# A new hand-over order and a new choice of engines for the 2,407 works of an attention and two-layer expert kernel

## The chip, the cores and the metric

The kernel runs on one core of a Trainium2 chip. The metric is the device time of one launch in microseconds. Before the change it is 660.46 us, the median of three runs (659.9 to 663.03).

## The reference: what is computed

Attention over 4 batches of 8 heads, 576 positions and 64 columns per head: heads 0 to 3 look at the last 32 positions, heads 4 to 7 at every fourth of the last 128. Its output, 2,304 tokens by 512, goes through a layer of 1,024 columns with a SoLU and a layer norm, and through a second one of 2,048 columns with a sigmoid GELU. All in float32; the four expert weights come as float64.

```python
scores = np.where(masks, q @ k.T / 8, -1e9)
x = softmax(scores) @ v                       # to (2304, 512)
h = x @ w_in;   s = h * softmax(h)
y = ((s - mean(s)) / sqrt(var(s) + 1e-6) * g_ln) @ w_out
h2 = y @ w2_in; g = h2 * sigmoid(1.702 * h2)
out = g @ w2_out
```

## The kernel before

**Works and queues.** The kernel body does not issue instructions as it goes. It fills a `Plan` (lines 61 to 163) with 2,407 works by `add` (line 67): an engine, a cost in us, a function that issues the instructions, the works it comes after, and the buffers it takes and gives back. A work can have further engines (`also`); which of them it gets is PICKS[number] (0, the first, where nothing stands). ORDER is a list of all work numbers written out by hand, found by a search outside of the kernel. `in_order` (line 78) walks it, gives every work a start time by the costs in the code, and `emit` (line 150) issues the works in order of these times, chained per engine in that order. So on each of TensorE, VectorE, ScalarE, GpSimd and SP (which issues every DMA) the works run strictly in the order in which ORDER names those of that engine; a work whose operands are late holds up all behind it on its engine. Works on GpSimd, and VectorE works marked `port`, also follow one another in the planner's times, as both read through a shared port.

**Attention** is 20 units (`n` = 5 x batch + u): u = 0 to 3 are two heads each with 512 positions, u = 4 the last 64 positions of all heads. A unit goes through `att_s` (scores, TensorE, line 258), `att_max` and `att_sub` or `att_mask` (VectorE), `att_exp` (ScalarE, line 318), `att_sum` (three VectorE instructions, lines 339 to 341), `att_norm` (GpSimd, for some VectorE, line 344), `att_t` (transposition, TensorE, line 348), `att_p` (copy out of PSUM, ScalarE or VectorE, line 357), `att_x` (times v, line 362) and two `att_y` copies.

**First expert layer.** 18 tiles of 128 tokens. Float32 products are made of three products of split operands: a rounded high part and the rest, the low part (`moe_xh`, line 505, and `moe_xl`, line 511, for tokens; `split_hi`, line 477, and `split_lo`, line 490, for weights, which `to_f32_*` first turns from float64 to float32). `moe_h` (line 517) is two halves of twelve products; then come maximum, exponential, SoLU, mean, variance and norm (`moe_ln`, GpSimd), the transposition `moe_lt` (line 572) and `moe_y` (line 593), 24 products for each of four column blocks of six groups of three tiles.

**Second expert layer.** Three passes (p = 0 to 2) of 768 tokens, by a scheme with seven products for a 2 x 2 block (m = 0 to 6) in both matrix products. Its weights ("units", 32 of them) are fetched, converted, summed (`unit_sum`), split (`unit_hi`, `unit_lo`) and stored to DRAM during the first layer, and loaded back per pass (`quad_load`, `o_load`, `o_load2`; the tiles ws, wo and w). `y_sum` (line 691), `y_hi` (line 700) and `y_lo` (line 705) make the seven token operands of a pass. `h_prod` (line 710) and `o_prod` (line 785) are six TensorE instructions each; `o_sum` (line 754), `o_hi` (line 761) and `o_lo` (line 765) make the operands of `o_prod` from the GELU's output; `h_u2` to `h_c12` add the products up in VectorE.

**Dummy products.** In the attention and in `moe_h` a helper issues bf16 products that nobody reads, as many as the planner's gap ahead of the work says:

```python
def stir(bank):
    x = ident_b.rearrange("p (o n) -> p o n", o=1).broadcast_to([P, 4, P])
    for _ in range(min(4, int(STIR * plan.gap / 4))):      # STIR = 7
        nc.tensor.matmul(bank.rearrange("p (o n) -> p o n", o=4), ident_b, x, start=True, stop=True)
```

The lines that take the order and the choice of engine:

```python
pick = PICKS.get(len(self.works), 0) if ORDER else pick           # line 70
one = [list(can)[pick]] if pick >= 0 else list(can)
for k, n in enumerate(ORDER):                                     # line 81
    w = self.works[n]
    (w.eng, (w.cost, w.fn, port)), = w.can.items()
```

Of the kernel before, what the change touches and what calls it, by code (L numbers as in the profile page):

```python
# [60 lines left out]
class Plan:  # L61
# [5 lines left out]
    def add(self, rank, eng, cost, fn, after=(), take=(), give=(), lag=None, also=(), port=False, pick=-1):  # L67
        lag = {"PE": 0.2, "POOL": 0.1}.get(eng, 0.06) if lag is None else lag
        can = {eng: (cost, fn, port and eng != "ACT" or eng == "POOL")}
        can.update({e: (c, f, port or e == "POOL") for e, c, f in also})  # L70
        pick = PICKS.get(len(self.works), 0) if ORDER else pick
        one = [list(can)[pick]] if pick >= 0 else list(can)
# [31 lines left out]
    def order(self):  # L104
        if ORDER:
            return self.in_order()
# [1179 lines left out]
def plan_sequence():  # L1286
# [29 lines left out]
    for b in range(1, B):  # L1316
        todo, k = items[b - 1], 0
        for u in range(UB):
# [47 lines left out]
ORDER = [8, 1, 56, 57, 58, 59, 4, 77, 0, 46, 78, 79, 47, 48, 60, 61, 80, 81, 49, 50, 5, 67, 68, 9, 266, 82, 83, 10,  # L1366
# [245 lines left out]
```

## Time and profile before

| | |
|---|---|
| median of three runs | 660.46 us (659.9 to 663.03) |
| the profiled execution | 656.88 us |
| its span, first to last instruction | 655.1 us |
| TensorE busy | 632.4 us, 97% of the span |
| VectorE, ScalarE, GpSimd busy | 448.4, 353.8 and 307.1 us |
| DMA | 163.53 MB, 250 GB/s in the mean |
| chain that ended last | TensorE 81%, VectorE 6%, DMA 5% |

How to read it: busy times overlap, so TensorE's 97% says that the end is set by what lies between its products, and where. The busy time of an engine with a lower share matters only where another engine waits for it. A line "A <- B" in the list of waits gives how long engine A stood until B released it.

### The profile page before, as it was taken

Reading aid. Unit: us, or ns where it says so; the run is one execution under the profiler, and the core shown is the slowest. Engines: PE = TensorE matmul, PEld = TensorE weight load, DVE = VectorE, ACT = ScalarE, POOL = GpSimd, SP = SyncE. Lnnn points to the kernel's source line nnn. Section 1 sums busy time; section 2 is a strip of 40 time slices with the busy share of each in tenths; the row PEclk is TensorE's granted clock in tenths of the full one; section 3 lists DMA queues with packets and bytes.
Section 4 is the critical chain, followed back from the end, with each engine's and each line's share of the span. In section 5 each row is a group of like instructions: output and inputs, shape, how many; then the busy total and the mean of one; then the engine's idle time right before and its main releaser. Section 6 shows DMA issues by size and latency. Waiting matters only on the chain.

```text
span 655.1 us, 14276 instructions
## 1 busy us (share of the span) xinstructions
PE 632.4 (97%) x5587; PEld 590.4 (90%) x5587; DVE 448.4 (68%) x736; ACT 353.8 (54%) x757; POOL 307.1 (47%) x348
## 2 busy tenths in 40 slices
PE   6799999999999999999999999999999999999997
PEld 3467889888989899999999999999999899999997
DVE  4898987685686857577877879434577754265663
ACT  4778884664475675645556755224456432334552
POOL 2347575665664485552554034302547730134671
PEclk9899999999999999999999999999999999999999
DMA  8895943743326755887899998667789768868873
GB/s 328 332 349 219 333 160 111 272 157 124 138 111 226 252 197 187 294 310 262 284 333 345 339 351 300 194 227 256 250 284 313 265 219 246 287 203 300 273 246 109
DMA packets 65011, 163.53 MB, mean 250 GB/s; under 512 B 6960, under 2 KB 28592, under 8 KB 64944
## 3 DMA queue, kind: packets, MB, share of 16 engines
q1 hardware_dynamic: 64944, 162.62, 72.4%
q8 instruction: 44, 0.72, 0.4%
q14 instruction: 23, 0.19, 0.1%
HBM read 126.42 MB, written 36.18 MB: 248 GB/s over the span
## 4 chain that ended last, share of the span: by engine, by line
PE 81%; DVE 6%; DMA 5%; issue 3%; POOL 2%; ACT 1%; SPq 1%; ACTq 0%; DVEq 0%; POOLq 0%
PE y L599 15%; PE h L525 15%; PE hz L720 14%; PE oz L798 10%; PE hx L720 10%; PE ox L798 8%; PE lt L579 3%; DMA wo<-wdo 2%; DVE gs L766 2%; PE s L271 2%; PE xt L384 1%; PE xt L387 1%; DMA v<-in_v_dram 1%; PE ptp L354 1%; DMA wdo<-hl_('o', 3, 1)_1_4964 1%
## 5 line engine op out<-in xcount | busy, mean ns | idle before, releaser
L763 ACT CAST gs<-g 128x384 fp32r<-128x384 f32 x168 | 84.9, 513 | 73.9 <-PE oz L798 33.9
L766 POOL TENSOR_TENSOR gs<-g,gs 128x384 fp32r<-128x384 f32 x59 | 67.2, 1143 | 98.2 <-ACT gs L763 87.3
L720 PE MATMUL hz<-yc,ws 128*128 128x384 f32 x492 | 98.5, 335 | 0.5 <-DVE u L732 0.3
L599 PE MATMUL y<-ln_t,wo_h 128*128 128x384 f32 x384 | 98.6, 337 | 0.0
L766 DVE TENSOR_TENSOR gs<-g,gs 128x384 fp32r<-128x384 f32 x109 | 74.4, 699 | 33.5 <-ACT gs L763 33.0
L720 PEld LDWEIGHTS hz<-yc,ws 128*128 128x128 f32 x492 | 86.3, 188 | 1.6 <-DVE u L732 1.0
L759 POOL TENSOR_TENSOR g<-g,g 128x384 f32<-128x384 f32 x38 | 42.2, 1117 | 80.2 <-ACT g L749 51.8
L720 PE MATMUL hx<-yc,ws 128*128 128x384 f32 x369 | 74.8, 335 | 0.6 <-DMA ws<-wdq 0.5
L599 PEld LDWEIGHTS y<-ln_t,wo_h 128*128 128x128 f32 x384 | 68.9, 188 | 0.5
L720 PEld LDWEIGHTS hx<-yc,ws 128*128 128x128 f32 x369 | 64.8, 188 | 1.2 <-DMA ws<-wdq 0.8
L599 PE MATMUL y<-ln_t,wo_l 128*128 128x384 f32 x192 | 64.3, 335 | 0.0
L749 ACT ACTIVATE g<-g 128x384 f32<-128x384 f32 x72 | 36.1, 521 | 51.8 <-DVE g L739 21.2
L525 PE MATMUL h<-wi_h,xh 128*128 128x512 f32 x144 | 59.0, 409 | 0.0
L798 PE MATMUL oz<-gs,w 128*128 128x384 f32 x288 | 53.9, 338 | 3.0 <-DVE gs L766 3.0
L525 PE MATMUL h<-wi_h,xl 128*128 128x512 f32 x144 | 56.6, 393 | 0.0
L525 PE MATMUL h<-wi_l,xh 128*128 128x512 f32 x144 | 56.3, 391 | 0.0
L798 PE MATMUL oz<-gs,wo 128*128 128x384 f32 x288 | 55.2, 337 | 1.0 <-DMA wo<-wdo 0.9
L798 PE MATMUL ox<-gs,wo 128*128 128x384 f32 x288 | 55.1, 338 | 0.7 <-DMA wo<-wdo 0.7
L798 PEld LDWEIGHTS oz<-gs,w 128*128 128x128 f32 x288 | 50.0, 188 | 4.1 <-DVE gs L766 3.6
L798 PEld LDWEIGHTS oz<-gs,wo 128*128 128x128 f32 x288 | 50.2, 188 | 2.2 <-ACT hl_('o', 3, 0)_0_4868 L654 0.7
L798 PEld LDWEIGHTS ox<-gs,wo 128*128 128x128 f32 x288 | 50.2, 188 | 1.6 <-DMA wo<-wdo 1.0
L759 DVE TENSOR_TENSOR g<-g,g 128x384 f32<-128x384 f32 x58 | 40.4, 701 | 14.0 <-POOL gs L766 8.2
(415 smaller groups left out, 1216.7 us busy)
## 6 DMA issues: line engine op xcount, KB each, us to landing
wo<-wdo SPq DMA_DIRECT2D x48, 512.0 KB, 5.8
ws<-wdq SPq DMA_DIRECT2D x41, 512.0 KB, 5.6
w<-wdo SPq DMA_DIRECT2D x72, 256.0 KB, 5.6
ws<-wdq SPq DMA_DIRECT2D x41, 384.0 KB, 5.4
qk<-in_qk_dram SPq DMA_DIRECT2D x14, 528.0 KB, 5.8
v<-in_v_dram SPq DMA_DIRECT2D x14, 512.0 KB, 6.7
out_dram<-ob SPq DMA_DIRECT2D x11, 384.0 KB, 5.8
w_t<-in_w_in_dram SPq DMA_DIRECT2D x8, 512.0 KB, 9.4
```

What stands on the lines that cost most here:

```text
L271: nc.tensor.matmul(ps[QB * j:QB * j + QB, h, m * KW:m * KW + KW], q_[rows, c:c + QB], k_[rows, c:c + KW], start=not masked, stop=not maske ...
L354: nc.tensor.transpose(ps[:, j * P:j * P + P], t[:, 2 * j:2 * j + 2, :].rearrange("p m k -> p (m k)"), ident)
L384: nc.tensor.matmul(o, w, pt[rows, x:x + QB].rearrange("p (r t) -> p r t", r=4), start=True, stop=True, tile_position=(64 * par, 64 * h))
L525: nc.tensor.matmul(hps[i][:, half, :], x[:, kt, :], w[:, kt, fs], start=(kt == 0 and j == 0), stop=(kt == KT - 1 and j == 2))
L579: nc.tensor.transpose(ps[:, j, :], es[i][:, f * P:f * P + P], ident)
L599: nc.tensor.matmul(yps[g, dm][:, 0:TG].rearrange("p (t n) -> p t n", t=GT), w[:, f, ds_], x[:, :, f, :], start=(f == 0 and j == 0), stop=( ...
L720: nc.tensor.matmul(ps[:, 0:TB2], quad_weights(p, q, m, kk, a), yc2[m][:, x, kk, :], start=(m < 4 and kk == 0 and i == 0), stop=(kk == 1 an ...
L749: nc.scalar.activation(g_tile(q, 0, 0) if (half, b) == (0, 0) else src, src, AF.Gelu_apprx_sigmoid)
L759: eng.tensor_tensor(o_block(jj, *o), o_block(jj, *x), o_block(jj, *y_), op)
L763: nc.scalar.copy(gsp[jj, m][:, 0], o_block(jj, half, b))
L766: eng.tensor_tensor(gsp[jj, m][:, 1], o_block(jj, half, b), f32(gsp[jj, m][:, 0]), ALU.subtract)
L798: nc.tensor.matmul(ps, w, gsp[jj, m][:, x], start=m < 4 and first and i == 0, stop=last and i == 2, skip_group_check=True)
```

## The change

The lists ORDER and PICKS are replaced, and nothing else. No cost, dependency, buffer or function changes, so both kernels issue the same works. The heads of the lists, and the lines around the end of pass 1:

```diff
-ORDER = [8, 1, 56, 57, 58, 59, 4, 77, 0, 46, 78, 79, 47, 48, 60, 61, 80, 81, 49, 50, 5, 67, 68, 9, 266, 82, 83, 10,
-         97, 98, 267, 268, 269, 69, 70, 14, 71, 3, 262, 261, 6, 84, 85, 86, 263, 18, 7, 62, 272, 99, 264, 265, 271,
...
-         1961, 1962, 1934, 1960, 1963, 1924, 1920, 1921, 1918, 1922, 1964, 1965, 1966, 1979, 1935, 1906, 1907, 1980,
-         1981, 1908, 1868, 1940, 1947, 1925, 1926, 1990, 1992, 1984, 1985, 1986, 1936, 2033, 2030, 1937, 1996, 2031,
...
-PICKS = {75: 1, 76: 1, 95: 1, 96: 1, 115: 1, 136: 1, 144: 1, 160: 1, 171: 1, 179: 1, 190: 1, 193: 1, 204: 1, 215: 1,
...
+ORDER = [1, 8, 56, 57, 58, 59, 18, 87, 88, 89, 0, 46, 60, 61, 4, 9, 77, 47, 48, 90, 49, 62, 50, 51, 78, 10, 97, 52, 7,
+         53, 91, 266, 267, 268, 79, 80, 81, 82, 6, 272, 5, 67, 54, 269, 270, 63, 98, 83, 68, 55, 271, 99, 273, 69, 70,
...
+         1913, 1916, 1966, 1924, 1925, 1926, 1917, 1974, 1975, 1950, 1980, 1981, 1985, 1986, 1989, 2010, 1990, 1992,
+         1982, 1936, 1937, 1996, 1987, 1943, 1993, 1994, 1995, 2001, 1997, 2031, 1998, 1999, 2003, 2033, 2034, 1946,
...
+PICKS = {50: 1, 52: 1, 54: 1, 55: 1, 73: 1, 86: 1, 91: 1, 104: 1, 127: 1, 136: 1, 146: 1, 159: 1, 160: 1, 168: 1,
...
```

Read with the works' numbers: 0 to 45 are loads (8 is query 1, 1 the masks, 18 the last block of batch 0). 1908, 1917 and 1926 are `o_prod` of pass 1, m = 5, for groups 1, 3 and 5; 1925 is the `o_lo` that 1926 needs; 1980 and 1985 are `y_sum` 2 and 3 of pass 2; 1992, 1996, 1994, 2001, 1998 and 2003 are `h_prod` 0, 2, 1, 4, 3 and 5 of its first quad, and 1982 and 1987 the `y_lo` for products 3 and 5.

Works by engine: VectorE 674 before and 711 after, ScalarE 612 and 592, GpSimd 286 and 269, TensorE 496 and SP 321 both times.

| works | GpSimd to VectorE | VectorE to GpSimd | ScalarE to VectorE | VectorE to ScalarE | to GpSimd from ScalarE |
|---|---|---|---|---|---|
| `o_lo` (168) | 37 | 25 | | | |
| `o_sum` (96) | 28 | 11 | | | |
| `unit_sum` (128) | 26 | 30 | | | |
| `unit_lo` (64) | 12 | 19 | | | |
| `y_lo`, `y_sum` (33) | 10 | 2 | | | |
| `unit_hi` (64) | | 2 | 10 | 3 | 9 |
| `att_p`, `att_y` (60) | | | 16 | 11 | |
| `moe_lnh`, `moe_yc` (60) | | | 15 | 14 | |

The number of dummy products follows from the gaps that `in_order` finds: 25 before, 34 after.

## Rows read from the trace of the kernel before

**Rows 1.** Windows by stage: us, busy (count) PE, PEld, DVE, ACT, POOL; granted clock, DMA share, GB/s
```profile
20.00:60.00 40.00, 33.94 (x826) 25.69 (x827) 37.83 (x52) 29.80 (x58) 20.96 (x20) 0.91 0.86 327
60.00:276.00 216.00, 216.00 (x2311) 193.21 (x2309) 157.56 (x272) 136.54 (x311) 130.04 (x182) 1.00 0.56 193
0.00:60.00 60.00, 46.73 (x1176) 33.15 (x1177) 46.24 (x68) 39.45 (x90) 25.09 (x31) 0.91 0.88 332
300.00:400.00 100.00, 97.72 (x555) 95.77 (x554) 78.69 (x139) 57.60 (x117) 40.08 (x44) 1.00 0.94 325
530.00:652.00 122.00, 120.72 (x687) 118.52 (x685) 64.87 (x106) 48.88 (x103) 42.92 (x40) 1.00 0.75 240
```
**Rows 2.** TensorE's waits: who for whom; us in total, times, longest
```profile
PE oz L798 <- DVE gs L766: 3.0, 2, 2.6
...
PE oz L798 <- DMA wo<-wdo: 0.9, 2, 0.5
PE ox L798 <- DMA wo<-wdo: 0.7, 1, 0.7
```
**Rows 3.** Windows in the start, columns as in rows 1
```profile
0.00:38.00 38.00, 27.10 (x732) 17.84 (x732) 26.01 (x39) 22.51 (x56) 13.12 (x17) 0.87 0.89 329
28.00:30.00 2.00, 0.13 (x2) 0.10 (x1) 2.00 (x3) 0.81 (x4) 0.00 (x0) 1.00 0.14 45
32.00:34.00 2.00, 2.00 (x91) 2.00 (x85) 1.86 (x8) 1.96 (x2) 0.61 (x1) 0.50 1.02 401
```
**Rows 4.** TensorE's timeline in the start: start, us, instruction [idle before, releaser]
```profile
30.38 0.38 PE L253 MATMUL xt<-ident_b 128*128 128x512 bf16 x1 [2.26 <-ACT t L324]
...
37.89 0.54 PE L525 MATMUL h<-wi_h,xh 128*128 128x512 f32 x1
```
**Rows 5.** VectorE's timeline in the start
```profile
6.71 0.69 DVE L306 TENSOR_REDUCE mx<-s 128x8 f32<-128x512 f32 x1 [6.71 <-PE s L271]
...
10.82 0.68 DVE L339 TENSOR_REDUCE sx<-t 128x8 f32<-128x512 f32 x1
...
11.85 0.64 DVE L339 TENSOR_REDUCE sx<-t 128x8 f32<-128x512 f32 x1
...
25.42 3.32 DVE L494 TENSOR_TENSOR wi_l<-w_t,wi_h 128x1024 fp32r<-128x1024 f32 x1
...
30.96 1.23 DVE L494 TENSOR_TENSOR wi_l<-w_t,wi_h 128x1024 fp32r<-128x1024 f32 x1
```
**Rows 6.** GpSimd's timeline in the start
```profile
24.80 2.86 POOL L494 TENSOR_TENSOR wi_l<-w_t,wi_h 128x1024 fp32r<-128x1024 f32 x1
```
**Rows 7.** The chain that ended last, from 30 to 75 us: start, us, what
```profile
36.65 0.21 PE s L253
...
68.64 2.76 PE h L525 x12
```
**Rows 8.** Timelines of VectorE, GpSimd and TensorE where pass 1 ends
```profile
520.34 2.60 DVE L696 TENSOR_TENSOR y<-y,y 128x768 f32<-128x768 f32 x1
522.87 2.16 DVE L766 TENSOR_TENSOR gs<-g,gs 128x384 fp32r<-128x384 f32 x1
...
522.21 2.41 POOL L696 TENSOR_TENSOR y<-y 128x768 f32<-128x768 f32 x1
...
525.09 1.15 PE L798 MATMUL oz<-gs,w 128*128 128x384 f32 x5 [2.56 <-DVE gs L766]
```
**Rows 9.** Lines 696 and 707 (`y_sum`, `y_lo`): duration ns least/median/most, first and last start
```profile
L696 DVE TENSOR_TENSOR y_early<-y_early x5: 943/951/2607, 286.5 to 402.0; 128x768 f32<-128x768 f32 x5
...
L707 POOL TENSOR_TENSOR yc<-y,yc x5: 1842/1860/2227, 466.5 to 525.9; 128x768 fp32r<-128x768 f32 x5
```
**Rows 10.** Groups of instructions: count, busy us, mean ns, idle before
```profile
L766 DVE TENSOR_TENSOR gs<-g,gs 128x384 fp32r<-128x384 f32 x109 | 74.4, 699 | 33.5 <-ACT gs L763 33.0
L766 POOL TENSOR_TENSOR gs<-g,gs 128x384 fp32r<-128x384 f32 x59 | 67.2, 1143 | 98.2 <-ACT gs L763 87.3 <-PE hz L720 10.6
...
L703 ACT CAST yc<-y 128x768 fp32r<-128x768 f32 x7 | 5.7, 832 | 4.2 <-DVE y L696 4.2
```

282 rows, old and new, of tables (ORDER, PICKS) are left out of this document.

## The prediction, made before the changed kernel ran

> **What bounds the kernel now.** I read the busy time by stage first [rows 1]. From 60 to 276 us TensorE is busy all of the 216 us; it is idle 13.3 us before 60, 2.3 us from 300 to 400 and 1.3 us from 530 to 652, and the last 3 us are a store that an order can't shorten. The list of who waited for whom [rows 2] names the holes after 60 us: VectorE's splits of `o` operands cost 3.0 us, 2.6 of it in one wait near 524 us, and waits for the weight loads wo sum to 1.6 us. So a new order can win in three places only: the start, that hole, and the stage from 300 to 400, where the DMA engines are busy 0.94 of the time.
>
> The start is VectorE's: from 20 to 60 us it is busy 37.8 of 40 us [rows 1], up to 38 us 26.0 us [rows 3]. The first product of the expert layer, `moe_h` of tile 0, begins at 37.89 us, behind a wait of 2.26 us for ScalarE's exponentials of unit 4 [rows 4]. These need a maximum that stands in VectorE's queue behind the split `wi_l`; and that split, from 25.42, took 3.32 us where the next one of the same shape took 1.23 [rows 5], since GpSimd had begun a split of its own at 24.80 [rows 6]. The collision cost 2.1 us just where TensorE stood still: it was busy 0.13 of the 2 us from 28 to 30 [rows 3].
>
> **The change, part by part.** Only ORDER and PICKS differ: the same 2,407 works, costs and dependencies, in another order on each engine; 37 works more on VectorE, 17 fewer on GpSimd, 20 fewer on ScalarE.
>
> *The start.* The first fourteen loads on SP's queue are the same fourteen (the last-block load of batch 0, two transfers, goes from the 11th place to the 3rd; weight 2 and value 0 come forward; query 2, values 1 and 3 and weight 0 go back), so by the 14th the same bytes have come. VectorE has thirty works up to the low part of tile 0, which it now computes itself instead of GpSimd. By the lengths of rows 5 (0.69 for a pass over 512 columns, 1.05 for a sum with its two small steps, from 10.82 to 11.85, and 1.23 for a pass over 1,024 with two inputs): five maxima and a half-width one 3.9, two subtractions 1.4, five sums and a half-width one 6.0, three conversions and two low splits 6.2, eleven others at 0.69, or 0.4 for half widths, 6.4: 23.9 us. It starts at 6.71, so it ends at 30.6 if it never waits. The old order's work up to 38 us, counted so, is 22.1 us for 26.0 busy: collisions stretched it by 3.9. GpSimd's split of weight 1 now comes before VectorE's low splits, but VectorE's normalisations meet GpSimd's, so I leave the 3.9 in: the product begins at 34.5, 3.4 us sooner. Ends: 7.3 sooner with no stretch, 0.5 later with twice the stretch. I take 3.4, as the stretch is what a row shows. After 60 us TensorE has no idle time in which such a gain could vanish before 300 [rows 1].
>
> *Dummy products.* `stir` issues `int(7*gap/4)` bf16 products, at most 4, by the gap that the kernel's planner finds ahead of a TensorE work. The new order makes 34 instead of 25. Ahead of the first expert product both hide them in idle time; behind it nine stand in the open (units 9, 10, 11, 19 and tile 12) instead of one. One takes 0.21 us there [rows 7]: 8 x 0.21 = 1.7 us lost. Ends: 0, where TensorE would have waited anyway, and 1.9.
>
> *The hole at 524 us.* Where pass 1 ends and pass 2 begins, VectorE has a sum of `y` (work 1980) ahead of the split (1925) that TensorE's next product needs. The sum took 2.60 us and the split 2.16, beside GpSimd's own sum of `y` (2.41), and TensorE stood 2.56 us [rows 8]; an undisturbed sum takes 0.94 [rows 9]. In the new order 1925 stands ahead, and both sums (1980, and 1985, until now GpSimd's) follow on VectorE. What is late next: product 5 of the next pass's first quad. Ahead of it stand seven products of 1.04 us, 7.3 us of cover; its operand waits for a split 0.95, a sum 0.95 to 1.3, ScalarE's 0.83 [rows 10] and two splits on GpSimd of 1.86 each [rows 9]: 6.5 to 6.9 us, up to 7.9 if GpSimd's are disturbed. I leave 0.3 us: 2.2 us won. Ends: 2.6 won, and 0.5 lost if all of it collides anew.
>
> By the page "SBUF — State Buffer" of the Trainium skill, section "Who interferes with whom", VectorE and GpSimd share a port pair under an exclusive lock, so that the later of the two waits out the other's whole instruction. Two sums on one engine then can't meet each other, the 0.3 us would go, and the sum below would be 0.3 lower; the 0.94 and 2.60 agree as far as they go.
>
> *VectorE instead of GpSimd in the late passes.* Of 168 operand splits 37 go to VectorE and 25 come back, of 96 operand sums 28 and 11: net 29 works of 1.14 us on GpSimd become works of 0.70 us on VectorE [rows 10]. They lie beside TensorE's products: VectorE is busy 0.53 and GpSimd 0.35 of the time from 530 to 652 [rows 1]. Cost and gain nothing beyond the hole; if the cover fails, a late split is 0.7 us, and I allow three: 2.1 lost.
>
> *The stage from 300 to 400.* As many transfers, in an SP order that differs by a few places; group 6's weights come ahead of group 2's, and group 3, still last, begins one product (1.04 us) later. I take nothing, between 1.0 won (most of the wait for wo) and 1.0 lost (one more such wait).
>
> **Sum.** -3.4 + 1.7 - 2.2 = -3.9 us. The profiled execution took 656.88 us (its span 655.1 and 1.8 around it), so 653.0 in its terms. The median shown is 660.46, 3.6 above it; I carry that difference over: 656.5 us, 0.6% faster. About 0.5%, 3.3 us, is what a measurement of this kernel can tell from no change.
>
> **The rivals.**
>
> *VectorE bounds the first 80 us and gets more to do first (slower).* Counted as above, the VectorE work that stands in the order ahead of tile 1's first product is 48.0 us instead of 42.4, ahead of tile 3's 58.4 instead of 53.9. If TensorE follows VectorE, the start is 4.5 us later instead of 3.4 sooner: 4.5 + 1.7 - 2.2 = +4.0, 664.5 us. It decides where tile 3's first product begins after 68.64 us, as it does now [rows 7]. For it speaks the 37.8 of 40 us; against it, that much of the work moved forward is needed by later products only. Chance 0.19.
>
> *The start's gain is stopped at 300 us (no change).* That stage moves 325 GB/s at a DMA share of 0.94 [rows 1]; if its loads don't come sooner, TensorE waits for wo by as much as it is early: 1.7 - 2.2 = -0.5, 660.0 us. For it speak the waits for wo; against it, that before 276 us the DMA share is 0.56, so that the loads can move with the products. Chance 0.20.
>
> *The clock (no change).* TensorE's idle stretch from 28 to 30 us is followed by a granted clock of 0.50, the 1.2 GHz level, from 32 to 34 [rows 3], over before the first expert product. In the new order the wait ahead of unit 2's transposition lies nearer to that product. If it runs at half clock, its 2.76 us [rows 7] come once more: -3.9 + 2.8 = -1.1, 659.4 us. The Trainium skill, "TensorE: Matmul & The Clock Gate", Part 1, has an idle array fall to half rate until activity releases it; by that the halved stretch moves along with the wait. Chance 0.05.
>
> **How the numbers follow.** The forecast, that both gains hold, has 0.56. Its own range is 652.5 (the far end of the start) to 659.0 (stretch and late splits); about four fifths of it lie beyond the 0.5%, as the start's end reaches further than the others'. So faster 0.45; same 0.11 + 0.20 + 0.05 = 0.36; slower 0.19. The range for 8 in 10 goes from 652.0 to 664.5, up to the middle of the VectorE case.
>
> **What would show it.** Right: `moe_h` of tile 0 begins at 33 to 36 us and tile 3's at 64 to 67; under 0.6 us of idle time at the border of passes 1 and 2; no wait of TensorE over 1 us elsewhere after 60 us. Wrong: waits of TensorE between 60 and 276 us for VectorE or GpSimd (the first rival), waits for wo that sum to over 4 us (the second), a granted clock under 1.00 in tile 0's product (the third).

## The result, and the profile after

The new kernel takes 650.61 us in the median of four runs (648.81 to 652.14); the kernel before, beside it, 660.18. The ratio is 0.9877 with a 95% interval of 0.9828 to 0.9926. A second series of the new kernel (six runs, against 29 of the kernel before) gave 651.19 against 658.08 us, ratio 0.9878 (0.9856 to 0.9900). So the change gains 1.2%, some 8 us, where 0.6% was forecast. The profiled executions stand closer together, 652.14 and 656.88 us, because the one of before lies 1.2 us under the median of those 29 runs and the new one 1.5 us over its own.

First the windows by stage of the new kernel, columns as in [rows 1]:

```profile
60.00:276.00 216.00, 215.18 (x2346) 191.41 (x2339) 154.88 (x274) 130.99 (x291) 134.35 (x195) 1.00 0.60 204
0.00:60.00 60.00, 47.15 (x1138) 33.32 (x1138) 42.35 (x73) 37.91 (x89) 18.41 (x26) 0.89 0.87 318
300.00:400.00 100.00, 98.58 (x567) 97.96 (x566) 80.32 (x151) 58.35 (x119) 35.54 (x42) 1.00 0.92 319
520.00:530.00 10.00, 10.00 (x60) 10.00 (x59) 5.86 (x10) 4.22 (x8) 5.59 (x4) 1.00 0.56 185
```

TensorE is busy all of the 10 us where the hole was, and it gained 0.9 us from 300 to 400. Up to 60 us its busy time rose by 0.4 us only, and VectorE, which was to set the pace there, is less busy than before: 42.35 us instead of 46.24.

TensorE's list of who waited for whom, the longest:

```profile
PE xt L384 <- issue: 4.3, 2, 3.8
PE ptp L354 <- POOL t L346: 2.3, 1, 2.3
PE s L271 <- issue: 1.9, 2, 1.6
...
PE ox L798 <- DMA wo<-wdo: 1.3, 1, 1.3
...
PE lt L579 <- DVE y_early L603: 0.5, 1, 0.5
```

The wait for VectorE's `o` splits (3.0 us in [rows 2]) is gone. In its place on top stands "issue", a wait of TensorE for nothing that the profile shows. That line bears on the start, below. VectorE's and TensorE's timelines where pass 1 ends:

```profile
521.77 0.95 DVE L696 TENSOR_TENSOR y<-y,y 128x768 f32<-128x768 f32 x1
522.64 0.95 DVE L696 TENSOR_TENSOR y<-y 128x768 f32<-128x768 f32 x1
...
515.21 8.48 PE L798 MATMUL oz<-gs,w 128*128 128x384 f32 x48
523.53 1.23 PE L720 MATMUL hx<-yc,ws 128*128 128x384 f32 x6
```

Both sums now follow one another on VectorE at 0.95 us each, instead of 2.60 on VectorE and 2.41 on GpSimd [rows 8], and no product waits.

**A count that idle time does not give.** A product of 128x384 shows as 0.336 us long, but two neighbours start 0.173 us apart. A wait of up to 0.16 us is thus inside "busy", and every longer one loses 0.16 us of itself there. So I took, for every product, the distance to the start of the next, less the distance that its line has when nothing is late (0.173 us at lines 599, 720 and 798, 0.230 at 525, some 0.009 at the tiny products of the attention; a dummy product counts whole), and summed that by stage. The figure for the tiny products moves the first column up or down for all kernels alike. It is all the time that TensorE spends on anything but useful products, in us:

```
kernel                     0-60  60-276 276-300 300-400 400-520 520-530 530-640  after   sum
before                    34.69   13.91    0.10    4.18    1.59    2.89    2.49   4.01  63.86
new                       35.03   16.90    0.15    2.18    0.51    0.05    0.32   3.98  59.12
new, second profile       34.97   17.56    0.15    0.52    1.07    0.05    0.32   3.99  58.62
old first, new rest       37.32   14.96    3.29    2.60    0.85    0.05    0.32   4.44  63.81
old order, new late eng.  35.05   14.90    0.39    3.52    1.15    1.04    0.62   4.00  60.67
new order, old late eng.  35.22   17.03    0.23    2.79    7.48    1.01    5.71   7.28  76.77
new without nine dummies  35.05   17.62    0.15    1.38    0.52    0.05    0.32   3.99  59.09
new without dummies       33.55   14.47    0.15    0.21    0.56    0.02    0.62   3.66  53.24
```

The first two lines answer, for these two executions, the question where the time came from. Nothing came from the start. The stage from 60 to 276 us lost 3.0. All the gain, 8.1 us, lies behind 276 us: 2.8 in the hole, 2.0 in the stage from 300 to 400, and 3.3 in waits of 0.6 us and less from 400 to 520 and from 530 to 640, of which the list of waits shows less than half.

### The profile page after: what moved, and what is told of

The parts are those of the page before. It is cut to its first block, busy times and chain, and to the rows that moved or that the text cites. A ratio compares the mean times of both kernels' runs of the same rounds, so it can differ in the third digit from the quotient of the medians.

```text
span 650.4 us, 14261 instructions
## 1 busy us (share of the span) xinstructions
PE 631.7 (97%) x5596; PEld 592.6 (91%) x5596; DVE 436.1 (67%) x773; ACT 344.8 (53%) x737; POOL 265.7 (41%) x331
## 4 chain that ended last, share of the span: by engine, by line
PE 88%; DMA 7%; DVE 3%; POOL 1%; issue 1%; ACT 0%; SPq 0%; POOLq 0%; DVEq 0%; ACTq 0%
PE hz L720 15%; PE oz L798 15%; PE y L599 14%; PE h L525 14%; PE hx L720 12%; PE ox L798 11%; DMA w_t<-in_w_in_dram 3%; PE lt L579 2%; PE xt L387 1%; DMA wo<-wdo 1%; PE xt L384 1%; DMA y_early<-in_w_in_dram 1%; PE s L271 1%; DMA wdq<-park_hl 1%; PE ptp L354 1%; DMA qk<-in_qk_dram 1%
## 5 line engine op out<-in xcount | busy, mean ns | idle before, releaser
L766 POOL TENSOR_TENSOR gs<-g,gs 128x384 fp32r<-128x384 f32 x47 | 49.9, 1067 | 144.1 <-ACT gs L763 136.0
L766 DVE TENSOR_TENSOR gs<-g,gs 128x384 fp32r<-128x384 f32 x121 | 68.7, 590 | 28.1 <-ACT gs L763 26.3
L759 POOL TENSOR_TENSOR g<-g,g 128x384 f32<-128x384 f32 x21 | 22.8, 1089 | 66.4 <-ACT g L749 24.8
L759 DVE TENSOR_TENSOR g<-g,g 128x384 f32<-128x384 f32 x75 | 43.6, 597 | 7.6 <-POOL gs L766 5.8
```

The costliest lines, as they stand in the source:

```text
L759: eng.tensor_tensor(o_block(jj, *o), o_block(jj, *x), o_block(jj, *y_), op)
L766: eng.tensor_tensor(gsp[jj, m][:, 1], o_block(jj, half, b), f32(gsp[jj, m][:, 0]), ALU.subtract)
```

## The experiments

Theory A is this reading. Theory B is the forecast's: the start gains, and one stall in the profiled start of the new kernel was bad luck. ORDER and PICKS stand written out in each kernel, and so do the numbers of dummy products by work (DUMMIES), which the two kernels compute; the diffs give how these lists were made. OLD and NEW are the two orders.

**Halves exchanged.**

```diff
-ORDER = NEW
+ORDER = NEW[:950] + [w for w in OLD if w not in NEW[:950]]    # first run; the second has OLD and NEW exchanged
```

> The first 950 works (loads, attention, first expert layer, up to about 275 us) stand in the new order with the new engines, all others in the old order with the old engines; the number of dummy products is held at the new kernel's 34. Theory A, from a comparison of the two profiles product by product: up to 276 us the new order loses some 3 us (the start about even, the dummy products 2 us, small waits the rest), and its whole gain of 8 us lies behind. Then this kernel is 3 us (0.5%) slower than before, and its second part has the hole of 2 to 3 us near 524 us again. Theory B, the forecast's: the start gains 3.4 us and loses 1.7 on dummy products, and the one long stall in the new kernel's profiled start was bad luck. Then it is 1 to 3 us faster than before.

> The other way round: the first 950 works in the old order with the old engines and the old 25 dummy products, all others in the new order with the new engines. Theory A: 8 us (1.2%) faster than before and 3 us faster than the new kernel, with no wait of TensorE over 1 us behind 276 us apart from one for a weight load. Theory B: 2 to 3 us faster than before (the hole alone), so slower than the new kernel by 1 to 3 us at the least.

The new first half with the old rest: 660.95 against 658.08 us, ratio 1.0033 (1.0011 to 1.0055), by that 2.2 us slower. The old first half with the new rest: 654.38, ratio 0.9942 (0.9918 to 0.9965), 3.8 us faster. Each has a wait at its seam, where the halves meet, that neither parent has, first the one of the first run, then of the second:

```profile
PE y L599 <- DVE ln_t L589: 1.7, 1, 1.7
```

```profile
PE y L599 <- ACT y L603: 2.9, 1, 2.9
```

Without these the halves come to about +0.5 and -6.7 us. The times alone don't decide. The first run speaks against B, which had it 1 to 3 us faster. The second, 3.2 us over the new kernel in the median, came out as B had it, and comes near A's 8 us only with its seam taken off. The table decides for A: behind 300 us the kernel before loses 15.2 us, the new one 7.0 and this second run 8.3 (the first run, counted alike, 15.8). It adds something about the old start. It varies: 34.7 us lost in the profile that the forecast was made from, 35.1 in another, 37.3 in this run, where the mean granted clock up to 60 us is 0.86 instead of 0.91. The new start, its dummy products as they are, loses 34.9 to 35.2 in five profiles. The forecast's profile was a good one of the old start, and that is one reason why the medians stand further apart than the profiles.

**The border of the passes alone.**

```diff
-... 1980, 1981, 1908, 1868, 1940, 1947, 1925, 1926, ...
+... 1925, 1980, 1981, 1908, 1868, 1940, 1947, 1926, ...
```

> The old order and the old engines with one work moved: the split 1925 stands ahead of the sum 1980 on VectorE where pass 1 ends. If the hole near 524 us is the order of these two alone, it goes: 2.6 us (0.4%) faster than before, and TensorE has under 0.6 us of idle time from 520 to 530 us. If the sums of the next pass only move the wait (they are late for the products of its first quad), the same idle time stands some microseconds later, and the time is that of before to 1 us.

656.33 against 658.08 us, ratio 0.9962 (0.9936 to 0.9988): 2.5 us by the ratio, as expected of the hole. The window where it was:

```profile
520.00:530.00 10.00, 10.00 (x59) 10.00 (x59) 6.36 (x8) 3.60 (x7) 7.44 (x5) 1.00 0.81 276
```

This window is from its one profiled execution, at 663.62 us the longest of the twelve, so nothing else is read from that trace. One work moved past a sum gives a third of what the whole search gave.

**The same kernel again.**

> The new kernel unchanged, a second profiled execution. Theory A: the start shows the same stalls of TensorE in which no operand is late, 6 us in sum up to 66 us, the longest of 3 to 4 us near 17 us, and the first expert product begins at 39 to 41 us. Theory B: the 3.81 us stall was bad luck; it is under 2 us now and the product begins at 36 to 38 us.

Theory A. The stall near 17 us is there again (3.93 us, and 3.7 to 3.9 in four more profiles, though 2.8 and 2.4 in two others), and the first expert product begins at 40.02 us. It is no accident.

**The nine dummy products behind the first expert product.**

```diff
-    for _ in range(min(4, int(STIR * plan.gap / 4))):
+    for _ in range(plan.dummies):     # as before, but 0 for units 9, 10, 11, 19 and tile 12
```

> The new order and engines with the nine dummy products behind the first expert product left out (units 9, 10, 11 and 19, tile 12); the other 25 stay. Theory A: they stand in the open, 9 x 0.21 = 1.9 us, so this is 1.9 us faster than the new kernel (ratio to before 0.985 instead of 0.988). Rival: TensorE waits for the operand there anyway, or the waits behind them grow by as much; then the time is the new kernel's to 0.5 us and idle time stands where the dummy products stood.

The rival. 650.81 us, ratio 0.9874 (0.9840 to 0.9909): nothing gained, and the stage from 60 to 276 us loses 17.6 us (16.9 and 17.6 with them). In place of the dummy products other waits grew, spread over several lines. Two that show in its list:

```profile
PE lt L579 <- DVE y_early L603: 1.3, 1, 1.3
...
PE lt L579 <- POOL e L568: 0.3, 1, 0.3
```

**What the "issue" stalls are.** 64 tiny products on the identity are put ahead of the first scores:

```diff
             stir(ps[:, 0, :])
+            for e in range(64 if n == 1 else 0):
+                h, j = ((0, 0), (1, 2), (0, 1), (1, 3), (0, 2), (1, 0), (0, 3), (1, 1))[e % 8]
+                nc.tensor.matmul(ps[QB * j:QB * j + QB, h, 0:KW], ident[64 * h:64 * h + 64, 0:QB], ...
```

> The new kernel with 64 tiny products (64x32 by 64x64, nobody reads them) ahead of the first scores, while TensorE waits for query 1 anyway. Theory C: the stalls without a late operand (1.6 us near 11 us, 3.8 near 17, 0.6 near 27) are TensorE waiting for its next instructions, which come in blocks of 256 instructions (128 products). Then each stall comes 64 products earlier in the program: the second falls into the scores ahead, in the middle of unit 5, instead of the 33rd product with v of unit 0. Rival D: they are waits for something at that point in the program (a transfer, an engine that the list doesn't name); then they stay at the same products. In time C gives the new kernel's to 2 us either way, as the sum of the stalls may change; D gives 0.5 us more than the new kernel.

TensorE's timeline of the new kernel, then of the shifted one (lines of the source stand four lower in it):

```profile
10.36 0.72 PE L271 MATMUL s<-y_early 64*32 64x64 f32 x48
12.68 0.35 PE L271 MATMUL s<-y_early 64*32 64x64 f32 x16 [1.60 <-issue]
...
16.55 0.68 PE L384 MATMUL xt<-pt,v 64*64 64x32 f32 x33 [0.23 <-DMA v<-in_v_dram]
21.04 1.08 PE L384 MATMUL xt<-pt,v 64*64 64x32 f32 x31 [3.81 <-issue]
...
27.28 0.88 PE L387 MATMUL xt<-pt,y_early 64*64 64x32 f32 x42 [0.60 <-issue]
```

```profile
10.78 0.44 PE L287 MATMUL s<-qkl 64*32 64x64 f32 x8 [2.99 <-issue]
...
17.36 0.47 PE L275 MATMUL s<-y_early 64*32 64x64 f32 x16 [1.35 <-issue]
...
24.84 0.67 PE L388 MATMUL xt<-pt,v 64*64 64x32 f32 x31 [2.21 <-issue]
...
30.71 1.49 PE L391 MATMUL xt<-pt,y_early 64*64 64x32 f32 x42 [2.32 <-issue]
```

The run was ill-aimed: each of these products stands in the trace as two, as all tiny float32 products do (32 calls, 64 rows), so the shift was 128 and not 64. That is a whole block by C, and the stalls came back at the same products, which D has too. What C alone explains is the new first stall, inside unit 4's scores. Read the stalls as counts of products from the beginning: behind 223, 350 and 477 in the new kernel, behind 223, 351, 478 and 605 in the shifted one, and behind 222 and 350 in the kernel before, where other products stand there. The distance, 127 products with their weight loads, is 254 instructions; the page counts 44 packets of a queue "instruction" with 0.72 MB, 16 KB each, for 2 x 5,596 instructions of TensorE: 254 for each packet. The kernel without dummy products, below, moves the stalls by known numbers and decides for C. So do the transfers of that queue: in all fourteen traces every "issue" wait over 0.15 us of the first 70 us, save one, ends 1.2 to 1.7 us after the end of such a transfer. The time here is 654.81 us, ratio 0.9934 (0.9906 to 0.9961), 4 us worse than the new kernel; the four stalls shown sum to 8.9 us, the three of the new kernel to 6.0.

Why a block is late, the transfers of that queue in the new kernel's trace show: when TensorE began a block, when the transfer of the next began, and how busy the DMA engines were between:

```
new kernel: block begun us   7.02   12.68   21.04   27.28   34.91   40.67
  next one's transfer us    10.42   18.48   24.74   31.02   35.12   40.63
  share of DMA engines       0.97    1.03    1.03    1.03    0.16       -
```

Once begun, the transfer takes 0.9 to 1.1 us, and where TensorE had run out, it went on 1.4 to 1.5 us behind its end. What varies is the 3.4 to 5.8 us ahead of it, and these fall to 0.2 us and less in the last two columns, where the DMA engines had little to do. The three blocks that end in a stall were used up in 4.1, 4.5 and 5.6 us; their successors could be used 5.7, 8.4 and 6.2 us after they were begun.

**Traffic added where the queue was empty.**

```diff
     def unit_fetch(u, room):
...
+        if len(raws) == 1:
+            for k in range(8):
+                junk = dpool.tile([P, 1024], F32, tag=f"junk{k}", bufs=1, name=f"junk{k}")
+                nc.sync.dma_start(junk, v[k])
```

> The new kernel with eight copies of 512 KB from DRAM to DRAM put on SP's queue behind the first weight unit (27 us), where the new kernel's DMA engines fall idle from 34 to 47 us; nobody reads the copies. Theory G: TensorE's instruction blocks wait behind the data that is queued; in the new kernel a block is fetched 3.4 to 5.8 us after the one before it was begun while the DMA share is 1.0, and within 0.2 us where it is under 0.2 (blocks begun at 34.9 and 40.7 us). Then these two fetches come 3 us or more later, and TensorE stalls for 1 to 3 us without a late operand inside tile 0's products, near 40 to 46 us. Rival: the distance depends on what TensorE runs; then both fetches stay within 1 us and no such stall appears.

The two windows in question, of the new kernel and of this one, and this one's stall in tile 0:

```profile
34.00:40.00 6.00, 6.00 (x169) 4.50 (x166) 4.16 (x6) 3.60 (x7) 0.00 (x0) 0.54 0.06 21
40.00:46.00 6.00, 6.00 (x117) 4.65 (x116) 5.83 (x10) 4.43 (x13) 1.04 (x1) 1.00 0.84 302
```

```profile
34.00:40.00 6.00, 6.00 (x180) 4.73 (x172) 5.49 (x8) 3.82 (x8) 0.00 (x0) 0.72 1.03 395
40.00:46.00 6.00, 4.57 (x110) 3.25 (x109) 4.21 (x7) 3.27 (x12) 1.04 (x1) 1.00 0.96 338
...
41.74 0.50 PE L525 MATMUL h<-wi_l,xh 128*128 128x512 f32 x1 [1.43 <-issue]
```

Theory G. The transfers for the blocks begun at 34.9 and 39.9 us now start 4.3 and 5.9 us later (0.2 and 0 before), and TensorE stands 1.43 us between two products of one tile whose operands are all there. The one run took 655.16 us.

**The wait ahead of unit 2 filled, and then the best of both.**

```diff
-DUMMIES = {..., 72: 4, ...}
+DUMMIES = {..., 72: 12, ...}      # first run; the second: 72: 7, and the nine of above left out
```

> The new kernel with 12 dummy products instead of 4 ahead of the transposition of unit 2, where TensorE stands 2.3 us from 29.1 to 31.4 us for GpSimd's normalisation; the eight more take 1.7 us of that. Theory E: that idle stretch brings the granted clock of 0.50 from 32.7 to 39.5 us, in which the products up to tile 0 take twice their time; filled, the clock stays at 1.00 there and the first expert product begins 3 us sooner, 2 to 3 us faster than the new kernel. Rival: the half clock comes from what stood before (the 3.8 us stall), or the products then wait for VectorE; then the time is the new kernel's to 0.5 us.

> The new kernel with seven dummy products instead of four ahead of unit 2's transposition (twelve overshot: they ran at half clock until 31.8 us and held the transposition back by 0.9 us) and without the nine behind the first expert product. If the half clock between 32.7 and 39.5 us costs what it lasts, 2 us faster than the new kernel, 648.5 us. If VectorE's queue of weight splits ahead of tile 0's low part sets that product's start whatever TensorE's clock, the new kernel's time to 1 us.

The clock did what E says, the time did not. The stretch ahead of tile 0, first of the new kernel, then of the first run:

```profile
34.00:38.00 4.00, 4.00 (x101) 3.23 (x98) 3.93 (x5) 2.09 (x5) 0.00 (x0) 0.50 0.09 32
```

```profile
34.00:38.00 4.00, 3.43 (x144) 2.69 (x151) 3.93 (x5) 1.84 (x5) 0.00 (x0) 1.00 0.10 36
```

Then VectorE's `xh` (the high part of the tokens, the operand that the first expert product needs last) and that product, in the new kernel, the first run and the second:

```profile
36.98 0.42 DVE L508 CAST xh<-xr 128x512 fp32r<-128x512 f32 x1
39.79 0.58 PE L525 MATMUL h<-wi_h,xh 128*128 128x512 f32 x1
```

```profile
38.81 0.42 DVE L508 CAST xh<-xr 128x512 fp32r<-128x512 f32 x1
39.66 0.58 PE L525 MATMUL h<-wi_h,xh 128*128 128x512 f32 x1
```

```profile
37.25 0.42 DVE L508 CAST xh<-xr 128x512 fp32r<-128x512 f32 x1
37.72 0.50 PE L525 MATMUL h<-wi_h,xh 128*128 128x512 f32 x1 [0.18 <-DVE xh L508]
```

At 2.4 GHz instead of 1.2 the first run's product still begins at 39.66 (39.79 before), but `xh` comes 1.8 us later: in this execution the stall of 3.9 us had ended 1.0 us later, and the twelve dummy products overshot and held the transposition back by another 0.9. So this run does not show what the clock costs. The second comes closer. Its stall was shorter, 2.4 us, but its `xh` begins 0.3 us later than the new kernel's all the same, and at full clock the product begins 2.1 us sooner. In the new kernel TensorE works without a break from 32.87 to 39.79, nearly all of it at half clock, and ends 2.4 us behind `xh`.

The times do not show these 2 us. The first run took 649.75 us, ratio 0.9875 (0.9837 to 0.9913), the second 650.92, ratio 0.9875 (0.9848 to 0.9901): the new kernel's time both. The second's profiled execution, 648.71 us, was one of its best, and whether the clock stayed up in its others is not shown. In the ten runs of the new kernel the three with a mean granted clock of 0.992 or more took 648.81 to 649.68 us, the seven others 650.0 to 652.14; whether the clock makes the time, or the stalls make both, stays open.

**No dummy products at all.**

> The new kernel with none of its 34 dummy products. Theory H: the first expert product's start is set by the instruction blocks and by VectorE's queue of weight splits, and the dummy products only stand in waits; then the time is the new kernel's to 1 us (651 us), with as much or more time at the granted clock of 0.50 in the first 40 us. Rival: they hold the clock where it counts; without them the half clock reaches into tile 0's products and the time is 2 us or more over the new kernel's.

649.27 us (646.25 to 651.48), ratio 0.9840 (0.9808 to 0.9871): the lowest of all kernels here and 1.6% under the kernel before; against the new kernel 0.4%, with intervals that still overlap. Its first 60 us and its first expert product:

```profile
0.00:60.00 60.00, 44.72 (x1187) 34.92 (x1188) 44.95 (x76) 40.23 (x92) 20.55 (x29) 0.83 0.91 345
...
37.24 0.79 PE L525 MATMUL h<-wi_h,xh 128*128 128x512 f32 x1
```

Its three first stalls in TensorE's timeline:

```profile
12.45 0.32 PE L271 MATMUL s<-y_early 64*32 64x64 f32 x8 [1.70 <-issue]
...
20.03 0.54 PE L384 MATMUL xt<-pt,v 64*64 64x32 f32 x19 [2.13 <-issue]
...
26.52 1.06 PE L387 MATMUL xt<-pt,y_early 64*64 64x32 f32 x27 [2.56 <-issue]
```

Of the same three works 16, 31 and 42 products were left behind the stall in the new kernel; now 8, 19 and 27. The stalls have moved by 8, 12 and 15 products, and 8, 12 and 16 dummy products are missing ahead of them. A wait for something at that point of the program (D) would not move: these are the ends of instruction blocks.

The clock is lower than in any other run (0.83), and the product begins 2.5 us sooner. The rival's fear did come true in its letter, as the first two products ran slow (0.79 and 0.49 us), but it cost 0.3 us. Against a better place of the block boundaries as the reason speaks that the stalls ahead of the product sum to 7.8 us here, against 6.0. What the trace does show is the dummy products' own time. VectorE's maximum that began at 26.28 us in the new kernel, and TensorE's dummy products ahead of its scores there, then the maximum here:

```profile
22.05 1.89 PE L253 MATMUL ptp<-ident_b 128*128 128x512 bf16 x4
```

```profile
22.79 0.69 DVE L306 TENSOR_REDUCE mx<-s 128x8 f32<-128x512 f32 x1 [0.63 <-PE s L271]
```

It begins 3.5 us sooner, 1.0 of it because the stall ahead ends sooner; four dummy products at half clock had taken 1.89. The next stalls, 2.56 and 1.45 us, took a part of it back.

**Engines in the late passes.** The 113 works of `o_lo`, `o_sum`, `y_sum` and `y_lo` that changed their engine, put back in the new order, and put alone into the old one:

```diff
-PICKS = NEW_PICKS
+PICKS = {**NEW_PICKS, those of the 113 works as in OLD_PICKS}    # second run: old order, old picks, the 113 as new
```

> The new order, with the 113 works of o_lo, o_sum, y_sum and y_lo that changed their engine put back on their old one; the 34 dummy products stay. Theory F: GpSimd's 1.1 us instead of VectorE's 0.6 is what made TensorE wait 0.2 to 0.9 us a dozen times behind 276 us, and the new choice of engine is what took these waits away: then 3 us or more of them come back, and the time is 0.5% to 1% over the new kernel's. Rival, the forecast's: on either engine the work is covered, and the order alone took the waits away; then the time is the new kernel's to 1 us.

> The reverse of the run before: the old order, with the 113 works of o_lo, o_sum, y_sum and y_lo on the new kernel's engines; the old 25 dummy products. Theory F, that the choice of engine alone takes the small waits behind 276 us away: 2 to 5 us faster than before. Rival: order and engines were searched as a pair, and either half alone is worse than both kernels; then this is slower than before by 5 us or more, with waits of TensorE for splits on VectorE and GpSimd in the second part.

The new order with the old engines: 671.13 us, ratio 1.0196 (1.0161 to 1.0232), 20 us over the new kernel. The old order with the new engines: 654.72 us, ratio 0.9936 (0.9911 to 0.9962), 4.2 us under the kernel before. So the choice of engine is worth 4 us by itself, of which the table has 1.9 in the hole (the second sum of `y` is now VectorE's) and 2.7 in the other stages behind 276 us; and the new order leans on it. The waits of the first of the two:

```profile
PE ox L798 <- DVE gs L766: 4.3, 7, 1.1
...
PE oz L798 <- DVE gs L766: 2.5, 5, 1.4
PE oz L798 <- POOL gs L766: 1.9, 3, 1.0
```

What the engines do to each other is in the mean of one split, first in the new kernel, then in the new order with the old engines:

```profile
L766 DVE TENSOR_TENSOR gs<-g,gs 128x384 fp32r<-128x384 f32 x121 | 68.7, 590 | 28.1 <-ACT gs L763 26.3 <-POOL gs L766 1.5
...
L766 POOL TENSOR_TENSOR gs<-g,gs 128x384 fp32r<-128x384 f32 x47 | 49.9, 1067 | 144.1 <-ACT gs L763 136.0 <-DMA wdq<-hl_('q', 5, 1)_1_4496 3.2 <-DVE gs L766 3.1
```

```profile
L766 DVE TENSOR_TENSOR gs<-g,gs 128x384 fp32r<-128x384 f32 x109 | 82.2, 775 | 30.4 <-ACT gs L763 28.7 <-ACT g L749 1.5
```

A split that meets nothing takes VectorE 0.55 us (the median in both): in the traces of these two kernels, of the one before and of the second run, none that overlaps no GpSimd instruction takes over 0.56. What the mean has over it is the cost of meeting GpSimd: 0.15 us x 109 = 16 us in the kernel before (0.699, [rows 10]), 0.04 x 121 = 4.5 us now, 0.22 x 109 = 24 us in this run.

## Why the forecast was right in sign and half in size

**The start, -3.4 us: failed.** The step was "The start is VectorE's", and with it "it ends at 30.6 if it never waits". Its terms were fair: VectorE was busy 22.7 us up to 38 us, even less than the 23.9 that I counted, and the 3.9 us of collisions that I left in are gone. But it waited for TensorE's products, 3.08 us until 22.16 and 2.50 until 26.28, and I had put that at nothing. TensorE had stood 3.81 us for instructions, and behind that came the four dummy products at half clock, 1.89 us, which I had called hidden. The two waits, and the low part of tile 0:

```profile
22.16 0.42 DVE L406 COPY xr<-xt 128x256 f32<-128x256 f32 x1 [3.08 <-PE xt L384]
...
26.28 0.69 DVE L306 TENSOR_REDUCE mx<-s 128x8 f32<-128x512 f32 x1 [2.50 <-PE s L271]
...
37.44 0.69 DVE L514 TENSOR_TENSOR xl<-xr,xh 128x512 fp32r<-128x512 f32 x1
```

So the low part ends at 38.13 instead of 34.5, and TensorE, at half clock, is later still: tile 0 begins at 39.79 (33 to 36 was to show me right) and tile 3 at 69.57 (64 to 67). Against the profile of before that is 1.9 us later instead of 3.4 sooner. How these 5.3 us divide among stalls, dummy products and clock is not shown: no run took the stalls away, the run without dummy products had more of them and began sooner, and the shifted run, with 9.2 us of them ahead of tile 0, began it 0.2 us later than the new kernel. The stall was in the profile of before too, as "issue" 1.7 and 1.5 us in TensorE's waits; I read neither. The Trainium skill, page "Runtime: NRT & Kernel Launch", section "Instruction fetch mechanics", has instructions come in blocks of 16 KiB (256 of them) while the one before runs, at a cost that is mostly hidden. The trace agrees on the size (44 packets, 0.72 MB) and not on the cost in this stretch, where it is 6.0 us.

The other steps:

- **Dummy products, +1.7 us.** The lower end of its range was right for the nine behind the first expert product: 0, as other waits grow in their place. That those ahead of it are all hidden in idle time was wrong.
- **60 to 276 us.** Forecast: that nothing in it changes but the dummy products. It lost 3.0 us more than the profile of before and about 2 more than the mean of three old ones, and taking the nine out gives none of it back. Without any dummy products the stage loses 14.5 us, as with the old order, though the other 25 all stand ahead of it. Waits for VectorE and GpSimd at the transpositions of line 579 are a part; the rest I leave open.
- **The hole, -2.2 us.** Right: -2.8 in the profile, -2.5 in the run with this edit alone. By the Trainium skill's rule of the exclusive lock ("SBUF — State Buffer", "Who interferes with whom") the 0.3 us that I left standing would go too; two sums at 0.95 us with no wait behind them agree. One reading of the old hole was wrong: the 2.60 us of VectorE's sum stood mostly beside GpSimd's two splits `yc`, 517.77 to 522.12, and only its end beside GpSimd's sum.
- **VectorE instead of GpSimd in the late passes, 0.** The second largest error: the two stages of the small waits gained 3.3 us, and that made up for most of the start's. These engines alone are worth 4 us, some 2 of them in the hole. I looked for cover in busy shares and in the list of waits, and these waits, 0.6 us and less, are mostly hidden in a TensorE that reads as busy.
- **300 to 400 us, 0 with 1.0 either way.** Gained 2.0 us in one profile and 3.7 in the other, more than the range allowed, though one wait for wo, 1.3 us, passed the 1 us that I had set as a sign.
- **The sum** of -3.9 stood against -4.7 between the profiled executions by luck: by the table it was 5.0 us too good ahead of 276 us and 5.9 too bad behind. The median, 650.61, lies 1.4 us below the range. I had carried over the 3.6 us between the median and the profile of before, but that profile was a good one of a start that varies by 3 us, and the new kernel's lay 1.5 us over its median.
- **The rivals.** VectorE's bound: its marker came true (tile 3 after 68.64 us), its mechanism did not, as VectorE was less busy. The gain stopped at 300 us: no, the waits there fell. The clock: 0.50 ahead of tile 0, and 1.00 in its product, where I had put the price. It delayed that product's start, by 2.1 us against the one trace in which the wait was filled and `xh` came as early; in the time no run shows it.

## What to carry to other kernels

Before any engine is called the bound of a stretch of tiny products, count TensorE's instructions there and look for waits marked "issue": here a block of 127 products that ran in 4 to 6 us was not refilled in time while the DMA engines were full. Measure what TensorE loses by the distance between the starts of its products, not by its idle time. An order and a choice of engines that were searched together are priced together: taken apart here, the late passes' engines alone gain 4 us on the kernel before, and the rest of the change without them loses 13.

## What was not expected of the hardware

- Instruction blocks queue behind data. In the first 35 us of the new kernel, with the DMA engines full, the transfer of the next block begins 3.4 to 5.8 us after the last one was begun and takes 1 us more, and a TensorE that stands goes on 1.4 to 1.5 us later; with them nearly idle it begins after 0.2 us. Eight copies of 512 KB were enough to put a stall into the middle of a tile.
- With no dummy products TensorE had half the clock for 20 of the first 38 us (14 in the new kernel), and still began its first expert product 2.5 us sooner; the kernel was not slower.
- The time of the kernel before varied more from run to run (654.0 to 662.3 us in 29 runs) than the new one's (648.8 to 652.1 in 10). The profiled starts in the old order had a mean granted clock of 0.86 or 0.91, those of the new kernel 0.89 both times.
